# Keys and queries padded to 128 rows by the host, one transfer per step

## The chip, the cores and the metric

The kernel runs on one core of one Trainium2 chip. A core has five engines with a queue each: PE (TensorE: matmuls, and PEld, its weight loads), DVE (VectorE), ACT (ScalarE), POOL (GpSimd) and SP (SyncE), which here only issues transfers. Sixteen DMA engines move data between the chip's memory (HBM) and the core's on-chip memory, whose tiles have up to 128 rows (partitions). The metric is the device time of one execution in microseconds (us); lower is better.

## The reference, cut to what matters

Three stages follow each other: an attention with a gated state, a soft mixture of experts with 32 slots, and a gated feed-forward layer.

```python
B, H, S, D = 4, 8, 768, 48
f = 1 / (1 + exp(-f_logit))
for t in range(S):                       # attention, per batch and head
    state = f[t, :, None] * state + outer(k[t], v[t])
    y[t] = q[t] @ state
x = y as (B * S, H * D) = (3072, 384)
logits = x @ phi                         # (3072, 32)
d = softmax of logits over the tokens;   slot_input = d.T @ x
slot_out[e] = relu(slot_input[e] @ w1[e]) @ w2[e]     # 8 experts of 4 slots, 1024 wide
c = softmax of logits over the slots;    x = c @ slot_out
out = (sigmoid(x @ w_gate) * (x @ w_val)) @ w_out     # 1536 wide
```

The weights of the last layer are 64-bit floats, which the kernel turns into 32-bit ones on the chip.

## The kernel before

**Steps.** The attention runs in chunks of 128 positions: 24 steps i, step i being chunk u = i // 4 of batch b = i % 4, with all 8 heads. The 48 values of a head lie on rows. Heads are held in pairs: head j of a pair has rows 64 j to 64 j + 47, so that rows 0 to 47 and 64 to 111 carry data. Rows 48 to 63 between them are never loaded, but some operations read rows 0 to 111 in one go, so they must hold finite numbers: the kernel sets rows 32 to 63 of each of the three `kq` tiles to zero once at the start (L437 for the tile of step 0, L452 for the other two).

**What one step loads.** All loads are issued on SP, in program order:

- `f`, the gate logits (L287): 128 rows of 1,536 bytes, 0.197 MB
- `kq`, keys and queries (`load_kq`, L289 to L295): two transfers, one for each head of a pair, each of 48 rows of 4,096 bytes, so 0.393 MB for both
- `raw`, a piece of the 64-bit weights of the last layer (L420): 128 rows of 3,072 bytes, 0.393 MB
- `v` (L240): 128 rows of 1,536 bytes, 0.197 MB
- `w`, a third of one expert's first matrix (L101): 128 rows of 4,096 bytes, 0.524 MB; three steps (7, 11 and 15) load two of them

`kq` and `f` have three buffers each; `f` is issued four steps ahead and `kq` three. The program issues, in stage i: `w`, `f` of step i+4, `kq` of step i+3, `raw` of step i+3, `v` of step i+2. A `raw` load waits until DVE has finished with the piece that was in its buffer (the last operation of that conversion is L115).

**What a step computes.** POOL clamps `f` (L299), ACT makes its softplus (L303, L304), PE sums it along the chunk with a triangular matrix (`prep_s`, L311), ACT takes exponentials (L317, L318). POOL multiplies the keys in place (`prep_k`, L327; for step 0 DVE does it) and DVE the queries (`prep_q`, L331). PE then forms the scores (`a_stage`, L350), DVE masks them (`m_stage`, L357), PE transposes the keys (`kt_stage`, L151) and makes the state (L368) and the output (L386, L398). Beside this run the logits of the mixture (`l_stage`, L168), its online softmax, and the conversion of one `raw` piece (ACT L424, DVE L110 to L115). In the program `prep_c` and `prep_s` run ahead of `a_stage` by three and two steps.

**After the attention.** SP loads the experts' second matrices, first four into memory that the attention's tiles give free (`w2p`, L104), then four into the buffers of `w1` (L104), then the last layer's output weights (L741). PE computes the experts (L700, L719), and from about 205 us the last layer, where the loads are over and PE works almost without a gap.

Of the kernel before, what the change touches and what calls it, by code (L numbers as in the profile page):

```python
# [17 lines left out]
B, H, S, D = 4, 8, 768, 48  # L18
DM = H * D
TH = 64  # L20
HP = H // 2
T = 128
NU = S // T
# [22 lines left out]
def body(ctx, tc, fn, fd, kqd, v, phi, w1, w2, wg, wv, wo, out_t):  # L46
    nc = tc.nc
    V, A, PE, PO, SP = nc.vector, nc.scalar, nc.tensor, nc.gpsimd, nc.sync
# [28 lines left out]
    def constants():  # L77
        V.tensor_reduce(sel, ident.rearrange("p (b s) -> p s b", s=NS), axis=AX.X, op=ALU.add)
        V.tensor_copy(q128, sel[:, None, :].to_broadcast([128, 4, NS]))
        for g in range(2):  # L80
            V.tensor_reduce(
                own[:, g:g + 1],
                ident0[:, 16 * g:16 * g + 144].rearrange("p (j c) -> p j c", c=36)[:, :, 0:SL],
                axis=AX.XY, op=ALU.add,
            )
        V.tensor_scalar(own, own, BIG, None, op0=ALU.mult)

    def load_phi():
        for j in range(2):
            for a in range(2):  # L90
                SP.dma_start(
                    phs[64 * j:64 * j + D, 2 * a:2 * a + 2],
                    phi.rearrange("(a j h e) s -> a j e h s", a=2, j=2, e=D)[a, j],
                )
# [3 lines left out]
    def load_w1(e, c):  # L98
        if c == 0:
            w1t[e] = wep.tile([128, KC, FF], F32, tag="we", name=f"w1_{e}")  # L100
        SP.dma_start(w1t[e][:, c], w1[e].rearrange("(c p) f -> p c f", p=128)[:, c])  # L101
# [23 lines left out]
    def attention_in(att, aps, slow):  # L125
        def at(shape, tag, dt=F32):
            return att.tile(shape, dt, tag=tag, name=tag)

        def pt(shape, tag, bufs=1, name=None):
            return aps.tile(shape, F32, tag=tag, name=name or tag, bufs=bufs)  # L130
# [17 lines left out]
        def kt_stage(k):  # L148
            ps = pt([128, HP, 112], "m", 2, "ktp")
            for h in range(HP):  # L150
                PE.transpose(ps[:, h], k[0:112, h], ident[0:112, 0:112])  # L151
            A.copy(kts, ps)

        def x_stage(i):
            yt = yts[i % 4]
            ps = pt([128, 2, 2, 112], "m", 2, "xtp")
            for h in range(HP):
                PE.transpose(ps[:, h // 2, h % 2], yt[0:112, h], ident[0:112, 0:112])
            x = xt[i] = xs[i % 5]
            for h in range(2):  # L160
                (V.tensor_copy if h and i == NSTEP - 1 else A.copy)(x[:, :, h], ps[:, :, :, 64 * h:64 * h + D])

        def l_stage(u):
            lps[u] = pt([128, T], "m", 2, "l")
            for bs in (slice(0, B - 1), slice(B - 1, B)) if u == NU - 1 else (slice(0, B),):
                for h in range(HP):
                    for b in range(B)[bs]:
                        PE.matmul(  # L168
                            lps[u][32 * b:32 * b + 32], phs[0:112, h], yts[b][0:112, h],
                            start=(h == 0), stop=(h == HP - 1), tile_position=(0, 32 * b),  # L170
                        )
# [21 lines left out]
        def d1b(u):  # L193
            if u:
                V.scalar_tensor_tensor(srun, srun, al[u], su.pop(u), op0=ALU.mult, op1=ALU.add)
            else:
                V.tensor_copy(srun, su.pop(u))
# [15 lines left out]
        def d2b(u):  # L213
            d2b_mm(u)
            d2b_add(u)
# [22 lines left out]
        def load_v(i):  # L238
            u, b = divmod(i, B)
            SP.dma_start(vts[i % 2], v[b, u * T:(u + 1) * T].rearrange("t (j c) -> t j c", j=2))  # L240

        def fast_steps():
# [9 lines left out]
            kq, rawt, ft = [None] * 3, [None] * 3, [None] * 3  # L252
# [35 lines left out]

            def load_kq(i):  # L289
                u, b = divmod(i, B)  # L290
                for j in range(2):
                    SP.dma_start(
                        kq[i % 3][64 * j:64 * j + D].rearrange("p k h t -> p (k h t)"),
                        kqd[u, b, j].rearrange("d k c -> d (k c)"),
                    )  # L295


            def prep_c(i):
# [134 lines left out]
            load_f(0)  # L433
            load_f(1)
            V.memset(sps[32:64], 0.0)
            for t in kq[0:1]:
                V.memset(t[32:64], 0.0)  # L437
            load_kq(0)
            load_raw(0)
            load_v(0)  # L440
# [7 lines left out]
            load_f(2)  # L448
            for t in ee + rr:
                V.memset(t[:, :, T:T + 1], 1.0)  # L450
            for t in kq[1:]:
                V.memset(t[32:64], 0.0)  # L452
            V.memset(aps_, 0.0)
            load_kq(1)
            load_v(1)
# [19 lines left out]
            for i in range(NSTEP):  # L475
                u, b = divmod(i, B)
# [55 lines left out]
        def slow_steps():  # L532
            wt = [at([128, HP, T], f"w{i}") for i in range(2)]
            kk = at([128, HP, T], "k")
            qq = at([128, HP, 2, T], "q")
            zps = [pt([128, 2, HP, D], f"z{i}") for i in range(2)]
            aps_ = [pt([128, 2, 2, T], f"a{i}") for i in range(2)]

            def slow_step(i):
                u, b = divmod(i, B)  # L540
                w = wt[1][0:112]
                for j in range(2):
                    d = slice(64 * j, 64 * j + D)
                    SP.dma_start(wt[1][d], fd[u, b, j])
                    SP.dma_start(kk[d], kqd[u, b, j, :, 0])
                    SP.dma_start(qq[d, :, j], kqd[u, b, j, :, 1].rearrange("d (h t) -> d h t", t=T))
                load_v(i)
                A.activation(w, w, AF.Exp, scale=-1.0)
                V.tensor_scalar(w, w, 1.0, None, op0=ALU.add)
                V.reciprocal(w, w)  # L550
                kt_stage(kk)
                vv, s, q = vts[i % 2], sb[i % 2], qq
                vo, vm = [t.rearrange("p j (h e) -> p h j e", e=D) for t in (vv, vts[(i + 1) % 2])]
                z = zps[b % 2][:, b // 2]
                with tc.For_i(0, T, 1) as t:
                    V.tensor_tensor(
                        z[0:112], z[0:112], w[:, :, bass.ds(t, 1)].to_broadcast([112, HP, D]), op=ALU.mult
                    )
                    for h in range(HP):
                        V.tensor_tensor(  # L560
                            vm[:, h], vo[:, h], (ident, wt[0].rearrange("p h t -> p (h t)"))[h % 2][:, None, bass.ds(t, 1)].to_broadcast([128, 2, D]),
                            op=ALU.mult,
                        )
                    for h in range(HP):
                        for j in range(2):
                            PE.matmul(
                                z[64 * j:64 * j + D, h], kts[:, h, 64 * j:64 * j + D],
                                vts[(i + 1) % 2][:, j, h * D:h * D + D],
                                start=False, stop=True, skip_group_check=True,
                            )  # L570
                    V.tensor_copy(s[0:112], z[0:112])
                    for h in range(HP):
                        PE.matmul(
                            aps_[h // 2][0:D, h % 2, :, bass.ds(t, 1)], s[0:112, h], q[0:112, h, :, bass.ds(t, 1)],
                            start=True, stop=True, skip_group_check=True,
                        )
                for h in range(2):
                    for g in range(2):
                        A.copy(yts[i % 4][64 * h:64 * h + D, 2 * g:2 * g + 2], aps_[g][0:D, h])

            V.memset(wt[1][32:64], 30.0)
            V.memset(kk[32:64], 0.0)
            V.memset(phs[32:64], 0.0)
            for t in zps + aps_:
                V.memset(t, 0.0)
            load_phi()
            constants()
            for t in [qq] + yts:
                PO.memset(t, 0.0)
            for p in range(E * KC):  # L590
                load_w1(*divmod(p, KC))
            r = wt[0].rearrange("p h t -> p (h t)")
            V.tensor_copy(r[:, 0:TH], ident[:, TH:T])
            V.tensor_copy(r[:, TH:T], ident[:, 0:TH])
            for i in range(NSTEP):
                u = i // B
                slow_step(i)
                if i == NSTEP - 1:
                    break
                x_stage(i)  # L600
                if i % B == B - 1:
                    l_stage(u)
                    d1(u)
                    d1e(u)
                    d2(u)
                    d1b(u)
                    d2b(u)
# [16 lines left out]
        mb, u = mrun[(NU - 1) % 2], NU - 1  # L624
# [337 lines left out]
```

## Time and profile before

| | |
|---|---|
| median of 3 runs | 406.56 us (405.28 to 408.78) |
| profiled execution | 407.34 us, of which 405.6 us from the first to the last instruction (the span) |
| busy share of the span | PE 90%, PEld 68%, DVE 55%, ACT 50%, POOL 43% |
| attention, from the first to the last scores (L350) | 11.5 to 158.4 us |
| the chain that ended last | PE 58%, DMA 21%, DVE 7%, ACT 5% |
| loads | 62.98 MB in 30,144 packets, DMA engines busy until about 207 us |

The profile gives the busy time of each engine, the span in 40 slices, a chain of waits that is followed back from the last instruction, the groups of instructions with what ended the idle time before them, and the transfers. Its DMA share is the mean busy share of 16 DMA engines; a share near 1 says that the engines had work all the time, not that they moved as much as they can: the GB/s beside it says that.

### The profile page before, as it was taken

The numbers are of one execution on the slowest core, as the hardware profiler recorded it, in microseconds if no ns is written. First come the engines' busy times: TensorE is split into PE (matmuls) and PEld (weight loads), VectorE is DVE, ScalarE is ACT, GpSimd is POOL, SyncE is SP. The second block draws the span as 40 slices with busy tenths as digits, with TensorE's granted clock in tenths as the row PEclk, the third lists the DMA queues.
The fourth block names the chain that finished last, engine by engine and source line by source line (L and its number), as shares of the span: only waits on it lengthen the run. The fifth ranks groups of instructions, "written<-read, shape, count | busy, mean of one in ns | idle before, by whom it ended". The sixth has DMA issues, their size and how long they took to land.

```text
span 405.6 us, 9421 instructions
## 1 busy us (share of the span) xinstructions
PE 365.0 (90%) x3758; PEld 274.8 (68%) x3758; DVE 224.9 (55%) x445; ACT 204.8 (50%) x424; POOL 175.6 (43%) x162
## 2 busy tenths in 40 slices
PE   3996999888898678899999699999999999999993
PEld 2875787666676556434356488888888888888882
DVE  5695797667777758834399943224224224224221
ACT  4675667666666553212287445444444444444440
POOL 5543544524362521000059474555555555555550
PEclk9997999999999989999999889999999999999997
DMA  7989899999999965899940002002002002002002
GB/s 208 264 233 289 266 259 330 312 281 295 260 311 276 280 190 179 252 376 374 393 163 2 1 0 80 0 0 79 0 0 79 0 1 79 0 0 79 1 1 87
DMA packets 30197, 63.66 MB, mean 157 GB/s; under 512 B 3392, under 2 KB 17984, under 8 KB 30144
## 3 DMA queue, kind: packets, MB, share of 16 engines
q1 hardware_dynamic: 30144, 62.98, 50.6%
q8 instruction: 31, 0.51, 0.6%
q14 instruction: 22, 0.18, 0.1%
HBM read 58.25 MB, written 4.72 MB: 155 GB/s over the span
## 4 chain that ended last, share of the span: by engine, by line
PE 58%; DMA 21%; DVE 7%; ACT 5%; issue 3%; POOL 3%; SPq 2%; POOLq 0%; DVEq 0%; ACTq 0%
PE oup L875 11%; PE oup L876 11%; PE oup L886 10%; DMA f<-fn 10%; PE gvp L849 7%; DMA w<-w 7%; PE s L311 4%; POOL f L299 2%; DMA v<-v 2%; DMA raw<-wg 2%; PE y L398 1%; PE ktp L151 1%; PE hp L700 1%; DVE wo L112 1%; PE sip L220 1%
## 5 line engine op out<-in xcount | busy, mean ns | idle before, releaser
L863 POOL TENSOR_TENSOR hl<-sg,hh 128x512 fp32r<-128x512 f32 x72 | 95.2, 1325 | 80.8 <-ACT hh L861 67.7
L859 DVE TENSOR_TENSOR sg<-sg,gvp 128x512 f32<-128x512 f32 x72 | 48.8, 685 | 95.0 <-ACT sg L854 90.5
L875 PE MATMUL oup<-hh,wh 128*128 128x512 f32 x216 | 85.5, 396 | 4.0 <-ACT hh L861 4.0
L876 PE MATMUL oup<-hh,wl 128*128 128x512 f32 x216 | 84.8, 393 | 0.0
L854 ACT ACTIVATE sg<-gvp 128x512 f32<-128x512 f32 x72 | 42.9, 597 | 81.5 <-PE gvp L849 81.5
L299 POOL TENSOR_SCALAR f<-f 128x384 f32<-128x384 f32 x24 | 30.0, 1252 | 70.3 <-DMA f<-fn 52.1
L886 PE MATMUL oup<-hl,wh 128*128 128x512 f32 x198 | 56.4, 394 | 0.1
L875 PEld LDWEIGHTS oup<-hh,wh 128*128 128x128 f32 x216 | 41.1, 190 | 13.4 <-ACT hh L861 4.3
L861 ACT CAST hh<-sg 128x512 fp32r<-128x512 f32 x72 | 44.2, 613 | 9.3 <-DVE sg L859 9.3
L311 PE MATMUL s<-tri,f 128*48 128x128 f32 x384 | 30.0, 303 | 20.0 <-ACT f L304 18.6
L876 PEld LDWEIGHTS oup<-hh,wl 128*128 128x128 f32 x216 | 41.0, 190 | 8.5
L886 PEld LDWEIGHTS oup<-hl,wh 128*128 128x128 f32 x198 | 37.5, 190 | 8.4 <-POOL hl L863 0.6
L327 POOL TENSOR_TENSOR kq<-kq,e 112x256 f32<-112x256 f32 x46 | 35.9, 799 | 14.9 <-ACT e L317 4.9
L311 PEld LDWEIGHTS s<-tri,f 128*48 128x48 f32 x384 | 22.8, 135 | 23.3 <-ACT f L304 15.3
L357 DVE TENSOR_TENSOR r<-a,mask 128x512 f32<-128x512 f32 x48 | 30.9, 685 | 12.5 <-PE a L350 10.4
L808 POOL TENSOR_TENSOR wl<-wo,wh 128x768 fp32r<-128x768 f32 (+1 forms) x7 | 12.8, 1827 | 54.3 <-PE gp L838 50.7
L849 PE MATMUL gvp<-cs,wh 128*128 128x512 f32 x72 | 29.0, 402 | 0.6 <-ACT wh L840 0.6
L849 PE MATMUL gvp<-cs,wl 128*128 128x512 f32 x72 | 28.7, 399 | 0.0
L398 PE MATMUL y<-r,v 128*48 128x128 f32 x384 | 27.1, 282 | 1.6 <-DVE r L357 1.4
L398 PEld LDWEIGHTS y<-r,v 128*48 128x48 f32 x384 | 20.4, 125 | 8.3 <-issue 3.5
L303 ACT ACTIVATE f<-f 128x384 f32<-128x384 f32 x24 | 12.6, 524 | 22.4 <-POOL f L299 22.4
L350 PE MATMUL a<-kq 48*64 48x64 f32 (+1 forms) x768 | 22.6, 255 | 0.8 <-issue 0.8
(150 smaller groups left out, 526.9 us busy)
## 6 DMA issues: line engine op xcount, KB each, us to landing
w<-w SPq DMA_DIRECT2D x24, 512.0 KB, 8.8
kq<-kq SPq DMA_DIRECT2D x48, 192.0 KB, 7.6
w2p<-w SPq DMA_DIRECT2D x4, 1536.0 KB, 7.5
f<-fn SPq DMA_DIRECT2D x24, 192.0 KB, 8.1
raw<-wg SPq DMA_DIRECT2D x12, 384.0 KB, 6.9
v<-v SPq DMA_DIRECT2D x24, 192.0 KB, 7.0
raw<-wv SPq DMA_DIRECT2D x12, 384.0 KB, 6.6
out_t<-os SPq DMA_DIRECT2D x17, 256.0 KB, 2.2
```

Of the source, the lines that this page charges most:

```text
L299: PO.tensor_scalar(ft[i % 3], ft[i % 3], FMIN, None, op0=ALU.max)
L311: PE.matmul(sps[64 * j:64 * j + D, h], w[:, h, j], tri, start=True, stop=True, skip_group_check=True,)
L327: eng.tensor_tensor(k[:, h], k[:, h], e[:, h, :, ::1 - 2 * h], op=ALU.mult)
L398: PE.matmul(yps[64 * h:64 * h + D, j, g], vv[:, j, c:c + D], rrs[j][:, g, h], start=(i < B and g == 0), stop=True, skip_group_check=True,)
L849: PE.matmul(p, gs[n, k][:, o:o + 128], cs[:, u].rearrange("p b t -> p (b t)"), start=True, stop=True)
L854: A.activation(sg, ps[0], AF.Sigmoid)
L859: V.tensor_tensor(sg, sg, p, op=ALU.mult)
L861: A.copy(h, sg)
L863: PO.tensor_tensor(l, sg, h.bitcast(F32), op=ALU.subtract)
L875: PE.matmul(ops[u][c], wh[k][:, fo, cc[c]], h, start=(f == 0), stop=False)
L876: PE.matmul(ops[u][c], wl[k][:, fo, cc[c]], h, start=False, stop=False)
L886: PE.matmul(ops[u][c], wh[k][:, fo, cc[c]], l, start=False, stop=False)
```

## The change

The host now lays keys and queries out over 128 rows: it pads the 48 values of each head with 16 zeros, so that the array `kq` has, per step, rows 0 to 47 and 64 to 111 as before, and zeros in rows 48 to 63 and 112 to 127. `load_kq` brings a step's 128 rows of 4,096 bytes (0.524 MB) with one transfer, whose shape is that of a `w` transfer. The three memsets on `kq` are gone, since the zeros arrive with the data. The last hunk of the loads is in the slow path, which these inputs don't enter.

```diff
             def load_kq(i):
                 u, b = divmod(i, B)
-                for j in range(2):
-                    SP.dma_start(
-                        kq[i % 3][64 * j:64 * j + D].rearrange("p k h t -> p (k h t)"),
-                        kqd[u, b, j].rearrange("d k c -> d (k c)"),
-                    )
+                SP.dma_start(kq[i % 3].rearrange("p k h t -> p (k h t)"), kqd[u, b].rearrange("p k c -> p (k c)"))
...
             V.memset(sps[32:64], 0.0)
-            for t in kq[0:1]:
-                V.memset(t[32:64], 0.0)
             load_kq(0)
...
                 V.memset(t[:, :, T:T + 1], 1.0)
-            for t in kq[1:]:
-                V.memset(t[32:64], 0.0)
             V.memset(aps_, 0.0)
...
-                    SP.dma_start(kk[d], kqd[u, b, j, :, 0])
-                    SP.dma_start(qq[d, :, j], kqd[u, b, j, :, 1].rearrange("d (h t) -> d h t", t=T))
+                    SP.dma_start(kk[d], kqd[u, b, d, 0])
+                    SP.dma_start(qq[d, :, j], kqd[u, b, d, 1].rearrange("d (h t) -> d h t", t=T))
...
-        "kq": np.ascontiguousarray(np.stack([kr.reshape(NU, B, 2, D, HP * T), heads_t(q)], axis=4)),
+
+        "kq": np.pad(
+            np.stack([kr.reshape(NU, B, 2, D, HP * T), heads_t(q)], axis=4),
+            ((0, 0), (0, 0), (0, 0), (0, 64 - D), (0, 0), (0, 0)),
+        ).reshape(NU, B, 128, 2, HP * T),
```

On SP's queue at the start, before; `f`, `kq`, `raw` and `v` are the tiles loaded, and the brackets hold what an instruction waits for (DMAHW0 to DMAHW7 are the eight counters on which transfers report their end, each used by every eighth transfer):

```order
L287 DMA f_142<-fn 128x384
L287 DMA f_141<-fn 128x384
L292 DMA kq_139<-kq 48x1024 [waits DVE_49]
L292 DMA kq_139<-kq 48x1024
L420 DMA raw_137<-wg 128x768
L240 DMA v_118<-v 128x384
L287 DMA f_140<-fn 128x384
L292 DMA kq_138<-kq 48x1024 [waits DVE_49]
L292 DMA kq_138<-kq 48x1024 [waits DMAHW0_49]
```

And the same place of the kernel after:

```order
L287 DMA f_142<-fn 128x384
L287 DMA f_141<-fn 128x384
L291 DMA kq_139<-kq 128x1024
L416 DMA raw_137<-wg 128x768
L240 DMA v_118<-v 128x384
L287 DMA f_140<-fn 128x384
L291 DMA kq_138<-kq 128x1024
```

The first two `kq` loads have lost their wait for DVE's memsets, and each is one row where there were two.

A step in the middle of the attention on SP's queue, before; `w` is a `w1` piece:

```order
L287 DMA f_140<-fn 128x384 [waits DMAHW4_49]
L292 DMA kq_138<-kq 48x1024 [waits DMAHW5_49,PE_49,Pool_49]
L292 DMA kq_138<-kq 48x1024 [waits DMAHW6_49,PE_49]
L420 DMA raw_136<-wg 128x768 [waits DMAHW7_49,DVE_49,Activation_49]
L240 DMA v_118<-v 128x384 [waits DMAHW0_49,PE_49]
L101 DMA w_1_454<-w 128x1024 [waits DMAHW1_49]
```

And a step in the middle after:

```order
L287 DMA f_141<-fn 128x384 [waits DMAHW7_49]
L291 DMA kq_139<-kq 128x1024 [waits DMAHW0_49,PE_49,Pool_49]
L416 DMA raw_137<-wv 128x768 [waits DMAHW1_49,DVE_49,Activation_49]
L240 DMA v_118<-v 128x384 [waits DMAHW2_49,PE_49]
L101 DMA w_2_728<-w 128x1024 [waits DMAHW3_49]
```

A step issues five transfers where it issued six, in the same order; each still waits for the transfer eight places ahead of it, and the waits on the other engines are the same.

## Rows read from the trace of the kernel before

**Rows 1.** The page: the span in 40 slices of 10.1 us.

```profile
PEclk9997999999999989999999889999999999999997
DMA  7989899999999965899940002002002002002002
GB/s 208 264 233 289 266 259 330 312 281 295 260 311 276 280 190 179 252 376 374 393 163 2 1 0 80 0 0 79 0 0 79 0 1 79 0 0 79 1 1 87
```

**Rows 2.** The chain that ended last: start us, us, what.

```profile
90.49 8.44 DMA f<-fn
...
136.31 10.26 DMA f<-fn
...
176.43 12.16 DMA w<-w
188.61 8.41 DMA w<-w
```

**Rows 3.** Waits from 56 to 147 us: total us, times, longest us.

```profile
POOL f L299 <- DMA f<-fn: 34.4, 10, 4.5
...
PE s L311 <- ACT f L304: 6.8, 7, 2.0
```

**Rows 4.** SP's own waits in the same stretch.

```profile
SPq L420 <- DVE wgv L115: 17.7, 12, 2.1
SPq L292 <- DMA w<-w: 13.8, 10, 2.2
```

**Rows 5.** Stretches: busy us (instructions), then granted clock, DMA share, GB/s.

```profile
8.25:10.50 2.25, 1.89 (x12) 1.49 (x14) 1.85 (x6) 0.82 (x2) 1.42 (x1) 1.00 1.03 196
10.50:13.25 2.75, 2.59 (x44) 2.00 (x40) 0.82 (x2) 1.57 (x4) 0.92 (x2) 1.00 1.06 395
44.71:67.55 22.84, 22.35 (x460) 17.28 (x458) 20.18 (x48) 17.05 (x41) 10.00 (x11) 1.00 0.93 263
67.55:146.43 78.88, 67.74 (x1353) 52.07 (x1351) 55.99 (x132) 50.32 (x121) 32.62 (x35) 0.98 1.00 289
87.25:90.25 3.00, 2.63 (x56) 2.12 (x60) 1.44 (x4) 2.73 (x7) 0.56 (x1) 1.00 1.05 236
92.25:94.25 2.00, 2.00 (x53) 1.72 (x50) 1.97 (x5) 1.97 (x5) 1.33 (x3) 1.00 1.04 398
94.50:97.50 3.00, 1.79 (x29) 1.37 (x28) 2.67 (x8) 1.54 (x5) 0.32 (x1) 1.00 1.02 229
176.00:194.00 18.00, 17.74 (x177) 6.77 (x168) 5.77 (x18) 3.65 (x6) 0.00 (x0) 1.00 1.07 373
```

**Rows 6.** The page's transfers: how many, KB each, median us to landing.

```profile
w<-w SPq DMA_DIRECT2D x24, 512.0 KB, 8.8
kq<-kq SPq DMA_DIRECT2D x48, 192.0 KB, 7.6
```

**Rows 7.** PE in order of time: scores (L350) of steps 5, 9, 21, 22.

```profile
44.71 0.90 PE L350 MATMUL a<-kq 48*64 48x128 f32 x32
...
67.55 0.90 PE L350 MATMUL a<-kq 48*64 48x128 f32 x32
...
146.43 0.90 PE L350 MATMUL a<-kq 48*64 48x128 f32 x32
149.04 1.08 PE L311 MATMUL s<-tri,f 128*48 128x128 f32 x16 [1.72 <-ACT f L304]
...
153.88 0.90 PE L350 MATMUL a<-kq 48*64 48x128 f32 x32
```

**Rows 8.** SP's issues in order of time, at the start and after the attention.

```profile
2.65 0.81 SPq L292 DMA_DIRECT2D kq<-kq  x2
...
155.47 13.48 SPq L104 DMA_DIRECT2D w2p<-w  x4
174.92 14.06 SPq L104 DMA_DIRECT2D w<-w  x12
```

**Rows 9.** DVE's first memset on `kq`, in order of time.

```profile
1.71 0.91 DVE L437 MEMSET kq<- 32x1024 f32 x1 [0.27 <-issue]
```

**Rows 10.** PE's first transpose, in order of time.

```profile
8.61 1.11 PE L151 MATMUL ktp<-ident,kq 112*128 112x112 f32 x4 [1.19 <-POOL mask L280]
```

## The prediction

> **What bounds the kernel now.** I read the slices of the span first. The DMA engines are busy at 0.8 to 1.0 nearly all the time until 207 us, but the rate beside it says something else: with the same busy share they move 260 to 330 GB/s in the attention and 373 to 393 at 172 to 202 us [rows 1]. Something in the attention's loads keeps the engines busy without moving much. The chain of waits comes next: from 67 to 147 us it goes mostly through transfers of 8 to 10 us, time in the queue included, and then through the expert weights [rows 2]. The waits say who feels it: POOL sits 34.4 us, ten times, waiting for `f`, and PE waits for the softplus made from it [rows 3]. Scores start every 5.71 us from step 5 to step 9 ((67.55 - 44.71) / 4) and every 6.57 us from step 9 to step 21 ((146.43 - 67.55) / 12) [rows 7]. In the first stretch PE is busy 22.35 of 22.84 us and the DMA share is 0.93; in the second PE has 11.1 us of idle time and the DMA share is 1.00 [rows 5]. So steps 9 to 21 are bound by the transfers, with PE some 13% behind them. After the attention the time is fixed work whose start moves with the attention's end: the second matrices are issued into memory that it gives free [rows 8].
>
> **Which transfer is slow.** SP's queue is served in order, so fast and slow stretches can be given to transfers. At the start the order is f, f, kq, kq, raw, v, f, kq, kq, v, raw, raw. Counting bytes from the first transfer, the second `kq` pair (bytes 1.57 to 1.97 MB) falls into 8.25 to 10.50 us, at 196 GB/s, and the `v` and `raw` behind it into 10.50 to 13.25 us, at 395 [rows 5]. In a middle step the same: 229 and 236 GB/s in stretches of 3 us that hold one `f` and one `kq` pair, 398 where `raw`, `v` and `w` go [rows 5]. Nor does size explain it: a `w` of 512 KB lands 8.8 us after its issue, half a pair, 192 KB, after 7.6 [rows 6]. Row length is not the reason, since `w` has rows of 4,096 bytes too; the difference is 48 rows against 128. How long does a pair take? 8.25 to 10.50 us moved 0.441 MB; taking the 0.048 MB beyond the pair at 395 GB/s (0.12 us) leaves 2.13 us. 87.25 to 90.25 moved 0.708 MB, 0.315 beyond the pair (0.80 us), leaving 2.20; 94.50 to 97.50 leaves 2.26. I take 2.2 us for 0.393 MB.
>
> [...]
>
> **The change, part by part.**
>
> One transfer of 128 rows: 0.524 MB, the shape of `w`. At 395 GB/s that is 1.33 us, at the 373 of the long stretch of second matrices 1.41 [rows 5]. The saving is 2.2 - 1.4 = **0.8 us** of the queue's time a step. Bounds: if a pair goes at the mixed stretch's mean of 233 GB/s it takes 1.69 us, saving 0.28; if all of rows 5's long stretch (78.88 us at 289 GB/s, 22.8 MB, 4.72 of it the twelve pairs) goes at 395 but the pairs, they take 33.1 / 12 = 2.76 us, saving 1.4. I take the middle, nearest to the three single readings.
>
> How much of 0.8 reaches the end? By the queue, a step of 6.57 becomes 5.77. By PE it can't fall much under 5.7 [rows 5, 7]. Two limits this close don't mesh without loss, the more as steps 11 and 15 load a second `w`; I take 5.87, that is 0.70 a step. Twelve steps give **8.4 us**.
>
> Step 21 to 22 takes 7.45 us, with PE waiting 1.72 us for the softplus of the last `f`, whose transfer took 10.26 us from issue, behind more than one `kq` pair [rows 2, 7]. One pair's 0.8 us less, not all of it on the path: **0.6 us**. The steps behind load nothing more in the attention.
>
> Steps 0 to 8: **nothing**. PE is 98% busy from step 5 to 9. Before that, `f` comes late because SP issues it late, and no `kq` stands between it and the transfers it waits for. If that cover is gone, four steps at 0.8 would add 3 us; the range takes it in.
>
> Start: the first `kq` issue comes about 1 us earlier, since it waited for DVE's memset, 1.71 to 2.62 us [rows 8, 9], and three memsets of 0.91 leave DVE. The first transpose waits for POOL's mask until 8.61, not for `kq` [rows 10]: nothing. Were that cover gone, the gain is at most 1 us.
>
> SP issues 24 transfers fewer, about 0.4 us each [rows 8]. SP waited on two other things, the conversion of `raw` (17.7 us) and the transfer eight places ahead (13.8 for `kq` behind `w`) [rows 4]; with five transfers a step instead of six, eight places are 1.6 steps instead of 1.33, so the second wait shrinks and nothing is held up longer. A freed issue slot is worth nothing while the queue is full.
>
> No wait is added. The key and query operations keep their shapes. Rows 48 to 63 were zeros and stay zeros.
>
> After the attention: no change in length; the second matrices start earlier by what the attention gained. From 172 to 202 us the queue is full [rows 1], and stays so, and its 20 us on the chain before PE's second expert product [rows 2] only shift.
>
> Sum: 8.4 + 0.6 = 9.0 us. The profiled execution took 407.34 us, 405.6 in the span; that gives 398.3. It lies 0.8 above the median of 406.56, from which the same sum gives 397.6. I forecast **398.0 us**.
>
> **Rivals.**
>
> *Slower: bytes decide.* The change adds 0.131 MB a step. If a 128-row `kq` went at the attention's mean of 289 GB/s and the pair does too, each of 24 loads costs 0.45 us more, 10.9 in all, some 13 loads of them in the bound stretch: +5.9 us, 412.5. The point from which it decides: the new transfer slower than 0.524 / 2.2 = 238 GB/s. Against it: `w` has its exact shape and shares the queue at 395 to 398. Chance 7%.
>
> *Hidden anyway.* PE or POOL wait for `f` for another reason, and the 0.8 us only lets the queue run dry sooner. Then 404 to 407. Against it: POOL's 34.4 us of waits end with a landing. Chance 5%.
>
> *Another gate takes over.* SP's in-order wait for DVE's conversion (17.7 us in twelve waits [rows 4]) sits ahead of `f` of two steps later. With the queue faster, `f` is issued when DVE lets it, and only the pair in front of it in the queue shrinks: 0.8 us in each chain from issue of `f` to its use, about two steps long. That is 0.4 a step, 12 x 0.4 = 4.8, so about 402.5. For it: the waits are spread over all steps. Against it: in steps 5 to 9 the same gate allowed 5.71. Chance 15%.
>
> *More than forecast.* The saving is 1.2 or more and PE alone sets the pace. Its busy time is 67.74 us in the twelve steps, 5.65 each; 12 x (6.57 - 5.65) = 11 us, steps 21 and 22 at the same pace 1.8 more: 394.5. Chance 15%.
>
> **How the numbers follow.** The forecast, with its own range of 395.5 to 401, has 58%. The range 393.5 to 403.5 takes in the last rival and most of "another gate", and leaves out the bytes case, the hidden case and the tails of the others, about 17%. About 1% is what a measurement of this kernel can tell from no change: under 402.5 counts as faster. Faster: 58 + 15 + about half of the gate's 15 = 80%. Same: the other half of it and the hidden case, 12%. Slower: 8%, the bytes case and 1 for a mishap that I don't see.
>
> **What would show it.** The stretches of 200 to 236 GB/s, one a step, should be gone, and the mean rate of steps 9 to 21 should rise from 289 to about 345 GB/s ((22.8 + 12 x 0.131) MB in 70.4 us) at a DMA share still near 1 or just below. POOL's waits for `f` from step 9 on should fall well under half of 34.4 us, steps should start every 5.8 to 5.9 us, and the second matrices should be issued about 9 us earlier than 155.47. From there to the end the length should not change. I am wrong if the rate still dips below 250 GB/s once a step (rows are not what made it slow), or if it does not dip and steps still take over 6.3 us (the queue was not the bound).

## The result

The changed kernel takes 391.85 us (median; 389.10 to 400.76) against 406.18 us of the kernel before in the same comparison: a ratio of 0.9615, 95% interval 0.9541 to 0.9689. A second comparison, made later beside an experiment, gave 393.65 against 405.63 us, 0.9761 (0.9701 to 0.9821). The ratios here and below compare fast executions alone and leave out those more than 1.5% above the fastest of their kernel (of the change's four, the one of 400.76 us), so they are not the quotients of the medians. The change makes the kernel faster by 2.4 to 3.9%, 12 to 14 us. I had forecast 398.0 us with a range of 393.5 to 403.5: the direction was right, the size was not. 391.85 lies below the range, and the second median, 393.65, just inside it.

The profiled execution took 391.59 us, 389.8 in the span. The slices of its span, to be laid beside [rows 1]:

```profile
PEclk9997899999999999999999899999999999999998
DMA  7779889999998977999700001002002002002002
GB/s 246 287 255 344 297 279 374 363 352 356 347 367 281 336 221 211 379 373 385 292 2 1 0 20 63 1 0 82 0 0 82 0 1 82 0 0 82 0 1 91
```

The DMA engines are about as busy in the attention as before, but from 58 to 117 us they now move 347 to 374 GB/s (281 and 336 in the two slices behind), where it was 260 to 330, and the last loads end some 15 us earlier. The next lines are stretches: from step 5 to 9, from step 9 to 21, and from step 9 to 17 (columns as in [rows 5]).

```profile
43.40:65.42 22.02, 22.02 (x461) 17.27 (x459) 19.46 (x44) 16.93 (x41) 10.81 (x12) 1.00 0.85 295
65.42:132.67 67.25, 64.58 (x1352) 50.59 (x1350) 60.27 (x135) 49.93 (x121) 34.42 (x35) 1.00 0.97 348
65.42:109.86 44.44, 44.10 (x918) 34.53 (x916) 40.77 (x93) 34.23 (x83) 23.30 (x24) 1.00 0.99 356
```

The first column of times is PE's: it is busy 22.02 of 22.02, 64.58 of 67.25 and 44.10 of 44.44 us. In [rows 5] it had 11.1 us of idle time from step 9 to 21. The starts of the scores (L346 now) and PE's order of time show the same:

```profile
43.40 0.90 PE L346 MATMUL a<-kq 48*64 48x128 f32 x32
...
65.42 0.90 PE L346 MATMUL a<-kq 48*64 48x128 f32 x32
...
132.67 0.90 PE L346 MATMUL a<-kq 48*64 48x128 f32 x32
...
139.02 0.90 PE L346 MATMUL a<-kq 48*64 48x128 f32 x32
```

Against [rows 7], step 5 starts 1.3 us earlier, step 9 2.1, step 21 13.8 and step 22 14.9. From step 9 to 21 a step takes 67.25 / 12 = 5.60 us; it was 6.57. What comes after the attention keeps its length: the second matrices are issued at 140.61 us (155.47 in [rows 8]), and from there to the end of the span it is 249.2 us against 250.1.

```profile
140.61 13.62 SPq L104 DMA_DIRECT2D w2p<-w  x4
160.19 13.94 SPq L104 DMA_DIRECT2D w<-w  x12
```

The waits from 50 to 140 us, in total us, times and longest, hold a surprise (the last line is one of SP's own):

```profile
POOL f L295 <- DMA f<-fn: 33.3, 12, 4.4
...
ACT f L299 <- POOL f L295: 6.4, 6, 1.9
...
PEld s L307 <- ACT f L300: 2.4, 3, 1.1
...
PE s L307 <- ACT f L300: 1.9, 3, 0.9
```

```profile
SPq L416 <- DVE wgv L115: 42.5, 16, 4.6
```

POOL waits for `f` nearly as long as before (34.4 us in [rows 3]). But little of it is passed on: ACT's wait for POOL is 6.4 us where it was 12.0 (from 56 to 147 us), and PE's wait for the softplus is 1.9 us where it was 6.8. And SP, which before waited for the transfer eight places ahead [rows 4], now waits for no transfer in this stretch, but mostly for the conversion of `raw`.

### The profile page after: what moved, and what is told of

It reads as the page before. It is cut to its first block, busy times and chain, and to the rows that moved or that the text cites. A ratio compares the mean times of both kernels' runs of the same rounds, so it can differ in the third digit from the quotient of the medians.

```text
span 389.8 us, 9338 instructions
## 1 busy us (share of the span) xinstructions
PE 360.0 (92%) x3758; PEld 272.7 (70%) x3758; DVE 227.9 (58%) x442; ACT 204.1 (52%) x424; POOL 178.1 (46%) x162
## 4 chain that ended last, share of the span: by engine, by line
PE 71%; DMA 9%; DVE 9%; ACT 3%; issue 3%; SPq 2%; POOL 1%; POOLq 0%; DVEq 0%; ACTq 0%
PE oup L867 12%; PE oup L868 12%; PE oup L878 10%; PE gvp L841 8%; PE s L307 6%; DMA w<-w 5%; DMA f<-fn 4%; PE y L394 4%; PE a L346 3%; PE ktp L151 2%; PE y L382 2%; PE xtp L158 2%; PE kv L364 2%; PE l L168 2%; PE hp L692 1%
## 5 line engine op out<-in xcount | busy, mean ns | idle before, releaser
L855 POOL TENSOR_TENSOR hl<-sg,hh 128x512 fp32r<-128x512 f32 x72 | 95.7, 1331 | 79.0 <-ACT hh L853 66.1
L295 POOL TENSOR_SCALAR f<-f 128x384 f32<-128x384 f32 x24 | 31.1, 1296 | 53.8 <-DMA f<-fn 46.0
L323 POOL TENSOR_TENSOR kq<-kq,e 112x256 f32<-112x256 f32 x46 | 36.9, 823 | 14.5 <-ACT e L313 7.4
L346 PE MATMUL a<-kq 48*64 48x64 f32 (+1 forms) x768 | 22.3, 255 | 0.0
L346 PEld LDWEIGHTS a<-kq 48*64 48x64 f32 x768 | 18.6, 137 | 4.7 <-issue 1.9
```

Of the source, the lines that this page charges most:

```text
L323: eng.tensor_tensor(k[:, h], k[:, h], e[:, h, :, ::1 - 2 * h], op=ALU.mult)
L346: PE.matmul(aps_[r:r + TH, j, g, h, TH * s:T], k[d, p, r:r + TH], q[d, p, TH * s:T], start=True, stop=True, skip_group_check=True, tile_po ...
L855: PO.tensor_tensor(l, sg, h.bitcast(F32), op=ALU.subtract)
```

## The experiments

**Which rows, or how many transfers.** My theory: a transfer that covers only one half of the rows is slow. Rivals: it is the number of transfers (six a step against five), the rows that each DMA engine gets, or the memsets at the start. Two kernels part the first two; both bring the padded 0.524 MB with two transfers. The first splits them by rows:

```diff
-                SP.dma_start(kq[i % 3].rearrange("p k h t -> p (k h t)"), kqd[u, b].rearrange("p k c -> p (k c)"))
+                for j in range(2):
+                    SP.dma_start(
+                        kq[i % 3][64 * j:64 * j + 64].rearrange("p k h t -> p (k h t)"),
+                        kqd[u, b, 64 * j:64 * j + 64].rearrange("p k c -> p (k c)"),
+                    )
```

> The changed kernel, with its 128 padded rows brought by two transfers again: rows 0 to 63 and rows 64 to 127. Same bytes as the change (0.524 MB a step), six transfers a step as before, no memsets. Theory (a transfer that covers only half of the rows is slow whatever it carries): a half of 64 rows takes about as long as one of 48, 1.1 us, the pair 2.2 us, and the time is that of the kernel before, 403 to 409 us, with a stretch near 240 GB/s in every step (0.524 MB in 2.2 us). Rival 'number of transfers' (six a step instead of five, eight in flight): also about 406, so this run alone doesn't part the two. Rival 'memsets and their wait at the start': 392, since they stay away here. Rival 'few rows for each DMA engine' (3 before, 4 here, 8 in the change): the pair takes 0.524 MB at 4/3 of the old rate, 2.2 us too or less, 400 to 406.

Measured: 425.08 us, ratio 1.0448 (1.0377 to 1.0520): not back to the kernel before but 19 us slower. The stretch from step 9 to 21 of its profile, whose execution took 428.09 us:

```profile
75.53:166.22 90.69, 75.49 (x1352) 58.01 (x1350) 60.32 (x133) 50.23 (x121) 35.99 (x35) 0.87 1.02 252
```

A step takes 7.56 us, at a DMA share of 1.02 and 252 GB/s. The same bytes, split by rows, cost 33 us more than the change. The size surprised me: I had expected a half of 64 rows to cost what one of 48 does.

The second kernel splits them into keys and queries, over all 128 rows:

```diff
-                SP.dma_start(kq[i % 3].rearrange("p k h t -> p (k h t)"), kqd[u, b].rearrange("p k c -> p (k c)"))
+                for k in range(2):
+                    SP.dma_start(kq[i % 3][:, k].rearrange("p h t -> p (h t)"), kqd[u, b, :, k])
```

> The changed kernel, with the keys and the queries of a step brought by a transfer each: two transfers of 128 rows of 2,048 bytes. Same bytes as the change, six transfers a step as before. Theory (the rows that a transfer covers): as fast as the change, 390 to 394 us, rates of 340 GB/s and more in every step. Rival 'number of transfers': back to the kernel before, about 406 us, with SP waiting for the transfer eight places ahead for 20 us and more in steps 9 to 21. Half the row length could cost a little by itself: up to 2 us.

Measured: 392.33 us, 0.9704 (0.9631 to 0.9777). Six transfers a step again, rows of half the length, and as fast as the change. SP's wait for the transfer eight places ahead, 13.8 us in [rows 4], is this:

```profile
SPq L292 <- DMA w<-w: 0.7, 1, 0.7
```

So that wait was a sign of the full queue and no cause. The number of transfers is out.

**The memsets.** The three memsets put back:

```diff
+            for t in kq[0:1]:
+                V.memset(t[32:64], 0.0)
             load_kq(0)
...
+            for t in kq[1:]:
+                V.memset(t[32:64], 0.0)
             V.memset(aps_, 0.0)
```

> The changed kernel with the three memsets on rows 32 to 63 of the key and query tiles put back, so that the first loads wait for DVE as before. Theory: they cost 0 to 1 us, 391 to 393, since the first transposes wait for POOL and DVE's product, not for the load. Rival 'the start': the 1.3 us by which step 5 came earlier in the changed kernel goes away, 393 to 394.

Measured: 394.45 us, 0.9695 (0.9627 to 0.9762). That is 2.6 us above the change's first median, too little to part from the spread, so I ran both once more, side by side.

> The changed kernel itself, beside the next one, on one chip, so that the two can be told apart. Every theory: its ratio again, 0.955 to 0.970 of the kernel before.

> The changed kernel with the three memsets on the key and query tiles put back, once more beside the change itself. The first comparison left 2.6 us between them, within its interval, while step 5 began earlier with the memsets (43.06 us) than without (43.40). Theory 'the memsets and their wait at the start are worth nothing': the two agree within 0.5%, 2 us. Rival 'they are worth part of the gain': this one is 2 to 3 us slower again, and its step 1 or step 5 begins later by as much.

Measured: the change 393.65 us (0.9761, 0.9701 to 0.9821), with the memsets 392.80 (0.9728, 0.9660 to 0.9795). The memsets and their wait are worth nothing that can be measured.

**Transfers by themselves.** This kernel plays groups of loads ahead of the attention, each group behind a memset that waits for the one before:

```diff
+    def rates():
+        scr = [wep.tile([128, KC, FF], F32, tag="we", name=f"scr{i}") for i in range(3)]
+        src = [kqd[n // B, n % B].rearrange("p k c -> p (k c)") for n in range(8)]
+        for rows in (((0, 48), (64, 112)), ((0, 128),), ((0, 64), (64, 128)), ((32, 96),), ((0, 64),), ((0, 112),)):
+            for n in range(8):
+                for a, z in rows:
+                    SP.dma_start(scr[n // KC][a:z, n % KC], src[n][a:z])
+            for t in scr:
+                V.memset(t[:, :, 0:1], 0.0)
...
```

> The changed kernel with a piece ahead of the attention that measures transfers by themselves: six groups, with nothing else in the queue, each waiting for the one ahead. Eight times a pair of 48 rows (rows 0 to 47 and 64 to 111); eight times 128 rows; eight times a pair of 64 rows (0 to 63 and 64 to 127); eight times 64 rows from 32 to 95; eight times rows 0 to 63; eight times rows 0 to 111; always rows of 4,096 bytes. Its total time means nothing. Theory by the rows of the trace before: 48-row pairs near 180 to 200 GB/s, 128 rows near 390. [...] Rival 'few rows for each DMA engine': rows 32 to 95 and rows 0 to 63 run alike. [...]

A stretch inside each group, in the order of the expectation; the last column is the rate:

```profile
4.00:16.00 12.00, 0.00 (x0) 0.00 (x0) 0.12 (x2) 0.00 (x0) 0.00 (x0) 1.00 1.03 218
18.00:26.00 8.00, 0.00 (x0) 0.00 (x0) 0.12 (x2) 0.00 (x0) 0.00 (x0) 1.00 1.03 410
28.00:44.00 16.00, 0.00 (x0) 0.00 (x0) 0.18 (x3) 0.00 (x0) 0.00 (x0) 1.00 1.03 234
46.00:50.00 4.00, 0.00 (x0) 0.00 (x0) 0.17 (x3) 0.00 (x0) 0.00 (x0) 1.00 1.03 410
51.50:60.50 9.00, 0.00 (x0) 0.00 (x0) 0.15 (x3) 0.00 (x0) 0.00 (x0) 1.00 1.04 205
62.00:73.00 11.00, 0.00 (x0) 0.00 (x0) 0.12 (x2) 0.00 (x0) 0.00 (x0) 1.00 1.03 275
```

The fourth and fifth group decide it. Both bring 64 rows of 4,096 bytes, and by the rival of few rows for each engine they run alike; rows 32 to 95 go at 410 GB/s, as fast as all 128, rows 0 to 63 at 205. What parts these two is not how many rows a transfer has but which; why it is these rows, no run here shows. In time, a pair of 48 rows takes 0.393 / 218 GB/s = 1.80 us, a pair of 64 rows 2.24, one of 128 rows 1.28.

The last group is another surprise: 112 rows go at 275 GB/s, so that 0.459 MB take 1.67 us where 128 rows take 1.28. Leaving 16 rows out costs 0.4 us. Whether it is which rows each engine gets, no run here shows.

**A step's loads by themselves.** Single transfers give 1.80 - 1.28 = 0.5 us a step, far too little for 0.97. The next kernel plays the whole mix of a step in the program's order, without computing:

```diff
...
+        for rows in ((), ((0, 48), (64, 112)), ((0, 64), (64, 128)), ((0, 128),)):
+            for n in range(6):
+                u, b = divmod(n, B)
+                SP.dma_start(part(4 * n), w1[n // KC].rearrange("(c p) f -> p c f", p=128)[:, n % KC])
+                SP.dma_start(part(4 * n + 1)[:, 0:DM], fn[b, u * T:(u + 1) * T])
+                for a, z in rows:
+                    SP.dma_start(part(4 * n + 2)[a:z], kqd[u, b, a:z].rearrange("p k c -> p (k c)"))
...
+            for t in scr:
+                V.memset(t[:, :, 0:1], 0.0)
```

> The changed kernel with a piece ahead of the attention that plays the loads of a step without any computing: four groups of six steps, each step in the program's order w, f, kq, raw, v (1.31 MB without kq); the first group without kq, the second with a pair of 48 rows (0.393 MB), the third with a pair of 64 rows (0.524 MB), the fourth with one transfer of 128 rows (0.524 MB). The total time means nothing. From single transfers, 410 GB/s for all but the pairs, 1.9 us a 48-row pair, 2.24 a 64-row pair: 3.2, 5.1, 5.4 and 4.5 us a step. Theory 'a half-row transfer costs more than its own time, because it puts the DMA engines out of step with each other and slows what stands beside it': the second group takes 5.6 us a step or more, the third 6.2 or more, the fourth 4.5. Rival 'the sum of the parts holds, and the steps of the kernel before were held up by something else too': 5.1, 5.4, 4.5.

A stretch inside each of the four groups:

```profile
6.00:22.00 16.00, 0.00 (x0) 0.00 (x0) 0.37 (x6) 0.00 (x0) 0.00 (x0) 1.00 1.03 394
28.00:57.00 29.00, 0.00 (x0) 0.00 (x0) 0.43 (x7) 0.00 (x0) 0.00 (x0) 1.00 1.04 291
62.00:99.00 37.00, 0.00 (x0) 0.00 (x0) 0.43 (x7) 0.00 (x0) 0.00 (x0) 1.00 1.04 271
103.00:127.00 24.00, 0.00 (x0) 0.00 (x0) 0.43 (x7) 0.00 (x0) 0.00 (x0) 1.00 1.04 398
```

The bytes of a step divided by the rate: 1.311 / 394 GB/s = 3.33 us without `kq`, 1.704 / 291 = 5.86 with the 48-row pair, 1.835 / 271 = 6.77 with the 64-row pair, 1.835 / 398 = 4.61 with one transfer of 128 rows. In the mix the pair of 48 rows costs 2.53 us, not the 1.80 it takes alone; the 64-row pair 3.44, not 2.24; the 128-row transfer 1.28, just what it takes alone. So the change saves the queue 5.86 - 4.61 = **1.25 us** a step, and 291 GB/s is nearly the 289 of [rows 5]. In the second group each step has one slow stretch of about 3 us: from 48 to 51 us the engines move 217, 206 and 189 GB/s, 0.61 MB, where the pair alone is 0.393 MB and takes 1.80 us by itself. What stands next to the pair in the queue goes slowly with it. How the loss is shared between the two, and whether engines out of step with each other are the cause, no run shows.

The mix does not give the whole 6.57 us of a step before. Twelve of its steps and the two second `w` are 21.5 MB, and in [rows 5] the engines moved 22.8 MB from step 9 to 21, so some 1.3 MB had been queued before step 9 (SP issued 21.3 MB within the stretch). The two second `w` add 0.22 us a step and the 1.3 MB, at 289 GB/s, 0.38: 6.46 in all.

**What sets the pace now.** Two kernels load more in steps 0 to 15: 128 rows of 512 values, and of 1,024, into memory that is written later.

```diff
                 once(load_v, i + 2)
+                if i < 16:
+                    dum = wgv[NG - 1, i % 2].rearrange("p c n -> p (c n)")[:, 0:512]
+                    SP.dma_start(dum, w2[i % E].rearrange("(p c) d -> p (c d)", p=128)[:, 0:512])
```

> The changed kernel with one more transfer in each of steps 0 to 15: 128 rows of 2,048 bytes (0.262 MB) that nobody reads, into memory that is written later. It asks how much of the queue's time is left free now. At 405 GB/s it takes 0.65 us of the queue a step. Theory 'PE sets the pace of steps 5 to 20 now' (PE 96% busy from step 9 to 21, 348 GB/s against 405 that the queue can do, so 0.79 us a step to spare): 391 to 395. Rival 'the queue still sets the pace': 11 steps or more at 0.65, 399 or more.

> The same with 128 rows of 4,096 bytes (0.524 MB), 1.3 us of the queue a step, more than the 0.79 that theory 'PE sets the pace' leaves free: the rest, 0.5 us in 11 to 13 steps, comes to 6 us, 397 to 401. Rival 'the queue sets the pace already': 1.3 in each of them, 405 or more.

Measured: 394.72 us (0.9801, 0.9697 to 0.9905) and 400.83 (0.9937, 0.9884 to 0.9990). Steps 9 to 17, for the smaller and the larger load; the same stretch of the change stands above (44.44 us, 356 GB/s):

```profile
64.06:111.52 47.46, 44.58 (x918) 34.65 (x916) 37.89 (x92) 34.28 (x83) 22.83 (x25) 1.00 1.03 389
```

```profile
67.85:118.47 50.62, 44.46 (x919) 34.54 (x917) 39.60 (x91) 34.39 (x83) 20.38 (x25) 1.00 1.03 400
```

PE's busy time is 44.1 to 44.6 us in all three. In the change it fills the stretch; the queue moves 356 GB/s of the 398 that the mix can do, so it has 5.56 x (1 - 356 / 398) = 0.59 us a step to spare. The larger load takes 0.524 / 398 = 1.32 us: 1.32 - 0.59 = 0.73 a step must show, and (50.62 - 44.44) / 8 = 0.77 does. The smaller takes 0.66, 0.07 over what is spare, but 0.38 shows: where the two limits meet, a step of this kernel did lose some 0.3 us beyond either. From step 9 to 17 PE sets the pace of the change, and the queue stands half a microsecond behind it.

**Another 48-row load.** The matrix `phi` comes in four transfers of 48 rows, and in the change PE still waits 2.48 us around them and runs at half clock for part of the time (the granted clock is 0.77 from 30 to 45 us, and the product behind that wait takes 1.95 us where the next one of its kind takes 1.08). I padded it too:

```diff
-        for j in range(2):
-            for a in range(2):
-                SP.dma_start(
-                    phs[64 * j:64 * j + D, 2 * a:2 * a + 2],
-                    phi.rearrange("(a j h e) s -> a j e h s", a=2, j=2, e=D)[a, j],
-                )
+        SP.dma_start(phs.rearrange("p h s -> p (h s)"), phi)
...
```

> The changed kernel, with the mixture's matrix phi treated in the same way: the host pads it to 128 rows, one transfer brings it instead of four, and the memset on its rows 32 to 63 goes. In the changed kernel the four issues take SP 2.91 us at 25.4 us and the f behind them is issued at 28.83; PE then waits 2.48 us for its softplus and runs at half clock until about 41 us, so that step 4 takes 11.5 us. Theory 'phi's issues make that f late': f is issued about 2.2 us earlier, the wait goes to under 0.5 us, the clock stays up, step 4 takes 6 to 7 us and the time is 386 to 388. Rival 'SP is held by the conversion of raw, and f comes late anyway': the wait stays over 1.5 us, 390 to 392.

Measured: 392.22 us, 0.9734 (0.9668 to 0.9799): nothing. The `f` was issued 3.2 us earlier (25.62 us), the clock stayed up this once (30 to 45 us, 1.00), and PE still waited:

```profile
33.88 1.08 PE L302 MATMUL s<-tri,f 128*48 128x128 f32 x16 [2.69 <-ACT f L295]
```

The steps ahead had come earlier too. The rival was right about the wait; step 4 took 8.8 us instead of 11.5, and in this profile that was lost behind the attention, at half clock (0.54 from 150 to 160 us). That the clock stayed up can't be put down to `phi`: in the last kernel below, with `phi` padded too, it is 0.77 again, and with the smaller extra load, without it, the product behind the wait for the softplus (1.69 us there) took 1.08 us, as here, and not the 1.95 of the change. This leads to the last two kernels. In the first two profiles of the change, the stretch from 150 to 160 us reads

```profile
150.00:160.00 10.00, 9.27 (x86) 4.29 (x86) 7.15 (x24) 2.31 (x8) 0.00 (x0) 1.00 0.97 337
```

```profile
150.00:160.00 10.00, 9.62 (x54) 5.06 (x58) 5.51 (x19) 1.67 (x5) 0.00 (x0) 0.52 0.89 309
```

and the first expert product takes 5.36 us in the one and 7.56 in the other. Multiplications that nobody reads, put where PE waits in steps 22 and 23 and behind them, might hold the clock:

```diff
                 cv[3]()
+                if i > NSTEP - 3:
+                    keep_warm(3, "s")
                 y_intra(i)
...
         x_stage(NSTEP - 1)
+        keep_warm(0 if slow else 4, "y")
         d1e(u)
```

> The changed kernel with ten more multiplications of the identity by itself, whose result nobody reads, where PE waits at the end of the attention: three ahead of the last product of steps 22 and 23, where it waits 0.65 to 0.88 us for DVE's mask, four ahead of the transpose that waits 1.13 us for the running maximum. In the second profile of the changed kernel the granted clock is 0.52 from 150 to 160 us and the first expert product takes 7.56 us, in the first profile 1.00 and 5.36. Theory 'PE's idle time in steps 21 to 23 makes the clock fall in some executions, and that is most of the spread of the changed kernel': the clock stays at 1.00 in 150 to 160, the product takes 5.4 us, median 389 to 391. Rival 'the fall has another cause': it shows up still, median 392 to 394.

> The same with the matrix phi padded to 128 rows by the host and brought by one transfer. With one transfer alone the attention's last scores came at 140.16 us against 142.86 and 141.71 in the two profiles of the change, but the clock fell to 0.54 in 150 to 160 and the first expert product took 7.62 us, so that nothing was left of it. Theory 'that gain is there and the clock took it': with the clock held, 387 to 389, 2 us below the kernel without it. Rival 'nothing in it': the same as that kernel.

Measured: 392.51 us (0.9629, 0.9570 to 0.9689; 388.55 to 396.95) and, with `phi` padded as well, 389.78 us (0.9576, 0.9524 to 0.9628; 387.15 to 393.73). Both profiles have the clock at 1.00 from 150 to 160 us, and the product takes 5.36. But the first kernel's executions spread as widely as the change's and its median is the change's, so "that is most of the spread" has fallen: one profile each shows a clock that held, not what the other executions did. The second kernel has the lowest median of all and is faster than the kernel before beyond doubt; whether it is faster than the change (first 0.9615, then 0.9761) these runs don't settle.

## Why the prediction was right and where it was wrong

**What bound it: right.** The queue was the bound from step 9 to 21, the 48-row pairs were what kept it slow (291 GB/s in the mix with them), and one transfer of 128 rows goes at the rate of the loads around it (398 GB/s in the mix with it, 394 without). The rate in steps 9 to 21 came out at 348 GB/s where I had said 345; that is partly luck, for it is 23.4 MB in 67.25 us and not the 24.4 MB in 70.4 us of the forecast. The dip below 250 GB/s in every step is gone: of the 67 stretches of 1 us from 65 to 132 us nine lie below it, in three places. The longest, from 118 to 123 us, has a DMA share of 0.64 and comes after SP issued nothing from 114.4 to 118.8 us, when it waited for the conversion.

**The saving of 0.8 us a step: too small.** This is the step of the sum that failed. The mix says 1.25. I read the pair's time from single slow stretches (2.1 to 2.3 us) and rounded the new transfer up to 1.4. In the mix the pair costs 2.53 us and the new transfer 1.28: what a pair costs together with its neighbours doesn't show when the neighbours are taken off at the full rate. The better reading was the one that I kept for the upper bound: the whole stretch's bytes, all but the pairs at the full rate, left 2.76 us a pair, a saving of 1.4. The 1.25 of the mix lies closer to it than to my 0.8.

**The 5.87 us a step: wrong because of it.** With 0.8 the queue's limit (5.77) and PE's (5.7) nearly met, and I added a loss for that. The loss is real where they meet (0.3 us in the kernel with the smaller extra load), but here they don't: by the mix the queue's limit is 4.6, or 4.8 with the two second `w`, while PE is busy for 64.58 / 12 = 5.4 us a step and waits for 0.2, and the steps run at 5.60. PE's limit was lower than my 5.7, too: its busy time in the twelve steps had been 67.74 us, at a granted clock of 0.98 [rows 5], and is 64.58 at 1.00. Twelve steps gave 11.6 us instead of 8.4 (they take 67.25 us here, and 66.0 to 68.0 in seven more profiles of kernels that load whole rows and nothing extra); of the 3.2 between, 1.2 is the loss that I had added, and 2.0 the saving of 0.8 that was too small.

**Steps 0 to 8 at nothing: wrong, 2.1 us.** Step 5 starts 1.3 us earlier, and steps 5 to 9 take 22.02 us instead of 22.84, which is PE's busy time to the last digit. PE at 98% was not full. I had put the price of that cover, 3 us, in the range, and 2.1 of it came. How much of this is the change's is open: in the same seven profiles, two of them with the memsets put back, step 9 starts anywhere from 62.0 to 66.1 us, always ahead of the 67.55 before.

**Steps 21 and 22: about right.** 7.45 became 6.35 us, 1.1 instead of 0.6.

**After the attention: right.** The length changed by 0.9 us, and PE's clock fits that: after a wait of 3.96 us early in the last layer PE ran at half clock (granted 0.50) from 231.3 to 237.0 us before, and from 216.5 to 219.2 us in the change's profile (0.50 too). The sum by the profiled executions: 2.13 + 11.63 + 1.10 = 14.86 us at step 22, the same at the second matrices' issue, and 0.9 behind it, make 15.8 us of span; I had 9.0.

**The start: right.** The memsets are worth nothing that can be measured.

**The rivals.** "Bytes decide" and "Hidden anyway" fell with the first trace. "Another gate" fell too, though it looked right in the waits: SP waited 42.5 us for the conversion in 50 to 140 us, and PE's waits for the softplus, which is what a late `f` costs, came to 1.9 us in all. "More than forecast" (394.5, 15%; its saving of 1.2 us or more lies between the 0.8 that I took and my upper bound of 1.4) is what happened, plus the steps before 9. With 1.25 in place of 0.8, the queue's 5.3 us a step would have lain under PE's 5.7, and this would have been the forecast.

**A sign that misled.** I had said that POOL's waits for `f` should fall well under half of 34.4 us. They stayed at 33.3. A wait counts only where someone behind it is short of work.

## What to carry to other kernels

Where transfers bound a stretch, look at which rows each of them covers before looking at bytes. Here a third more bytes over all 128 rows took half of the queue's time that two 48-row transfers had cost (1.28 us against 2.53), and the same bytes in two halves of 64 rows made the kernel slower than before (425.08 us). Price such a transfer in the mix that it stands in, from the bytes and time of a whole stretch, not from the stretch that it fills. Then take the next limit from the busy time of the next engine. In this kernel two limits lost time to each other (0.3 us a step) when they were 0.07 us apart, and hardly any (0.04) when they were 0.7 apart.

## What was not expected of the hardware

- Rows 32 to 95 load at 410 GB/s, rows 0 to 63 at 205, at the same size (that it would matter which rows are covered had been one guess of mine).
- Rows 0 to 111 load at 275 GB/s: a transfer of 112 rows takes 1.67 us, one of 128 rows of the same length 1.28.
- A 48-row pair costs 2.53 us of the queue among transfers of 128 rows, 1.80 by itself; a 64-row pair 3.44 and 2.24.
- The granted clock of PE behind the attention was 1.00 in one execution of the change and 0.52 in another, from 150 to 160 us (the second nearly all at half clock), after a stretch in which PE idles about a quarter of the time (busy 7.59 and 7.47 us from 140 to 150); the first expert product took 5.36 and 7.56 us.
